# Attention and a gated MLP on one core: the first pair's loads in another order, a shared buffer for q, four buffers of split p

## The chip, the core and the metric

The kernel runs on one core of a Trainium2 chip. A core has five engines with their own instruction queues: TensorE (PE in the profile; its weight loads are PEld) multiplies matrices into PSUM, VectorE (DVE), ScalarE (ACT) and GpSimd (POOL) work on vectors, and SyncE (SP) issues most of the DMAs. Each engine works through its queue in order and waits on semaphores for the others. The metric is the device time of one execution in microseconds (us).

## The reference

Inputs are q, k and v of 4 batches x 8 heads x 1152 rows x 64 columns, and two weight matrices of 512 x 2048 and 2048 x 512, all f32. q and k are drawn with a spread near 0.79.

```python
q_pool = q.reshape(B, H, S // 2, 2, D).mean(axis=3)          # two neighbouring rows of q are one
scores = scale * np.matmul(q_pool, k.transpose(0, 1, 3, 2))  # 576 x 1152 for each head
scores = scores - np.max(scores, axis=-1, keepdims=True)
attn = np.exp(scores)
attn = attn / (np.sum(attn, axis=-1, keepdims=True) + 1e-09)
o = np.matmul(attn, v)
x = o.transpose(0, 2, 1, 3).reshape(B * 576, 512)            # heads side by side
h = x @ w_in
g = h * (1.0 / (1.0 + np.exp(-1.702 * h)))
out = g @ w_out
```

## The kernel before

The 32 heads are taken as 16 pairs, four for each batch. A pair has nine tiles of 128 rows of pooled q against 1152 columns of k (four of one head, "A", four of the other, "B", and one, "L", with 64 rows of each), so 144 score tiles in all.

**Pairs 0 to 3** (`WHOLE`, `WIDE`) are computed in f32. q and k are transposed on PE (`qk_tr`, L540) and copied out of PSUM in six parts (`qk_ev`), scores are f32 matmuls (L646), p is transposed on PE (`w_tr`, L768) and copied (`w_ev`), and p times v is L791. Meanwhile the two weight matrices are loaded in 32 pieces and made ready: `w_low` (L295) and `w_bits` (L299) on DVE, `w_exp` and `w_sign` on ACT, `w_mul` (L309) on POOL, a column sum on PE (`w_sum`, L314), and then `w_hi` and `w_lo` split them into two f16 parts.

**Pairs 4 to 15** use split operands: a value is an f16 high part plus an f16 rest, and a product is three f16 matmuls. q's row sums (`q_add`) are made on POOL, `q_hi` and `q_lo` write the two parts into `qn`, and `q_tr` transposes them by DMA; k goes the same way. For each tile: scores (L675); the row maximum and scaled copy `p` (`row_max`, L689); `lift` on the maximum; exponentials in place (`exps`, L696); `p_hi`, the f16 high part, into a buffer `hl` (L258 on ACT, L260 on DVE); `p_lo`, the rest, into the same buffer (L730); then one DMA transposes both into `pt` (`p_tr`, L743), and p times v follows on PE (L756). L258, L260 and L262 are lines of the helper `copy`, so many operations share them.

**The MoE part** runs in 9 blocks of 256 rows: h (L978), tanh on ACT, a gate on DVE, a split (`g_hi`, `g_lo`, L1003), and the second product (L1014). Blocks of a batch can start when its four pairs are done, and PE fills its waits with them. The last three blocks come after all attention.

**What sets the order.** Every step is added to a list (`plan.add`) with its engine, a cost, a rank, the steps that it follows, and the buffers that it takes and uses. `Plan.order` walks through it as a list scheduler: it picks the step that can start first by its costs, and among those within `wait` of that, the one of lowest rank. So the dictionary `rank`, the costs, `sizes` (how many buffers of a name there are) and `movable` (which steps may go to a second engine) set the order of each engine's queue; on the chip, semaphores alone decide when a step starts. `p` has three buffers, `hl` three, `pt` three, the scores one accumulator of three PSUM banks, and the loaded q, k and the parts `qn` one each. A step that takes a buffer waits for the last user of the one used before in the same place: `p_hi` waits for the transposition of the tile three before it.

The first pair's loads are issued by SP (q: first half, the two last parts, second half) and ACT (both heads of k, `k_load`); its row sums run on DVE. A load of the next pair's q waits until `q_add` has read the former one.

Of the kernel before, what the change touches and what calls it, by code (L numbers as in the profile page):

```python
# [141 lines left out]
def kernel(  # L142
# [26 lines left out]
    nc = tc.nc  # L169
# [18 lines left out]
        w1=1473.9738382899, w1_rate=812.7284009533, w2=2479.3934706835, w2_rate=62.2658245112,  # L188
        w1_cut=1764.9519973162, w1_cut_rate=0.0018904172, w2_cut=-269.851473856, w2_cut_rate=5.6062016033,
        v_max=1069.7920417805, load=-241.3418019351, prep=871.7951150424, max=-2026.5182514592,  # L190
        exp=640.8579795756, p_hi=-262.2674051923, p_lo=1525.5748408629, pv=1102.6265648828, x=557.4542312295,
        recip=1463.0570012603, w_tr=723.1050232894, w_ev=763.8780959185, g=-2229.8362745818,
        pv_b=-1120.3629115427, max_b=1656.4714364309, p_lo_b=1449.9352033366, prep_b=-1716.5596499645,
        v=1349.3135761977, lift=-444.2192073566,
# [21 lines left out]
    qn = [const.tile([128, 2, NJ, 128], F16, name=f"qn{i}") for i in range(1)]  # L216
# [126 lines left out]
    for i in range(32):  # L343
# [10 lines left out]
        plan.add(("w_low", i), "DVE", 0.335, r, lambda i=i: w_low(i), [("w_load", i)], use=[raw], two=True)  # L354
# [49 lines left out]
    def heads(x, g):  # L404
        return x[g.b, 2 * g.pr:2 * g.pr + 2]

    def k_load(g):
# [6 lines left out]
        for a in range(2):  # L414
            nc.scalar.dma_start(out=t[:, a], in_=heads(k, g)[a].rearrange("(p r) d -> p r d", r=KR))
# [704 lines left out]
    with tc.manual_schedule():  # L1120
# [6 lines left out]
        for t in qn:  # L1127
            nc.gpsimd.memset(t[:, 1, :, D:], 0.0)
# [32 lines left out]
```

## Time and profile before

| | us |
|---|---|
| median of 3 runs (lowest, highest) | 795.61 (793.12, 797.49) |
| profiled execution | 796.71 |
| span of the profiled execution | 795.0 |
| PE busy (share of the span) | 754.4 (95%) |
| DVE busy | 584.7 (74%) |
| ACT busy | 569.2 (72%) |
| POOL busy | 286.0 (36%) |

The span reaches from the first instruction to the last. Busy times are sums over the whole span, and the stages differ: pairs 0 to 3 end near 165 us, pairs 4 to 15 near 665, and the rest is MoE alone. A line of the profile names an engine, a source line, an operation and its tiles as out<-in; "idle before" is how long the engine stood still ahead of it, and the arrow says what ended that. A gap is read by asking which engine was late, and then why that engine was.

### The profile page before, as it was taken

The numbers are of one execution on the slowest core, as the hardware profiler recorded it, in microseconds if no ns is written. First come the engines' busy times: TensorE is split into PE (matmuls) and PEld (weight loads), VectorE is DVE, ScalarE is ACT, GpSimd is POOL, SyncE is SP. The second block draws the span as 40 slices with busy tenths as digits, with TensorE's granted clock in tenths as the row PEclk, the third lists the DMA queues.
The fourth block names the chain that finished last, engine by engine and source line by source line (L and its number), as shares of the span: only waits on it lengthen the run. The fifth ranks groups of instructions, "written<-read, shape, count | busy, mean of one in ns | idle before, by whom it ended". The sixth has DMA issues, their size and how long they took to land.

```text
span 795.0 us, 16660 instructions
## 1 busy us (share of the span) xinstructions
PE 754.4 (95%) x6716; PEld 509.3 (64%) x6716; DVE 584.7 (74%) x984; ACT 569.2 (72%) x929; POOL 286.0 (36%) x168
## 2 busy tenths in 40 slices
PE   5999999999998999999998998899999999999998
PEld 3565555656766677666675675666776677766664
DVE  5878999898887988788788887788787776222222
ACT  5988889789796878784777977776888886232322
POOL 3242242225746346334445543474364541000000
PEclk9999999999999999999999999999999999999999
DMA  9436073359999999999999999999999989010000
GB/s 302 171 136 217 30 247 112 113 120 189 208 206 202 189 225 185 215 201 214 180 209 217 208 179 196 236 205 200 194 226 187 173 127 177 1 28 2 27 1 26
DMA packets 335645, 128.75 MB, mean 162 GB/s; under 512 B 310736, under 2 KB 320976, under 8 KB 335568
## 3 DMA queue, kind: packets, MB, share of 16 engines
q1 hardware_dynamic: 335280, 127.10, 77.4%
q8 instruction: 52, 0.85, 0.4%
q10 hardware_dynamic: 288, 0.59, 0.3%
q14 instruction: 25, 0.20, 0.1%
HBM read 45.09 MB, written 4.72 MB: 63 GB/s over the span
## 4 chain that ended last, share of the span: by engine, by line
PE 61%; DMA 15%; DVE 10%; ACT 4%; issue 4%; POOL 3%; SPq 3%; POOLq 0%; DVEq 0%; ACTq 0%
PE h L978 16%; PE o L1014 15%; DMA pt<-hl 10%; PE s L675 7%; PE pv L756 7%; PE s L646 5%; DVE p L689 4%; PE o L768 4%; PE pv L791 4%; POOL hl L730 2%; ACT hl L258 2%; PE tr L803 2%; DMA raw<-in_moe_w_out_dram 1%; PE h L314 1%; SPq L743 1%
## 5 line engine op out<-in xcount | busy, mean ns | idle before, releaser
L730 POOL TENSOR_TENSOR hl<-p,hl 128x1152 f16<-128x1152 f32 x79 | 200.9, 2547 | 169.3 <-ACT hl L258 134.6
L689 DVE TENSOR_SCALAR_CACHE_REDUCE p<-s,e_s 128x1152 f32<-128x1152 f32 x144 | 203.3, 1412 | 34.5 <-PE s L675 24.0
L1014 PE MATMUL o<-wbuf,g 128*128 128x512 f16 x864 | 205.3, 379 | 1.2 <-DVE g L1003 1.2
L978 PEld LDWEIGHTS <-wbuf 128*128 128x128 f16 x1728 | 167.4, 98 | 41.9 <-issue 5.7
L696 ACT ACTIVATE p<-p,nm 128x1152 f32<-128x1152 f32 x144 | 179.8, 1249 | 12.5 <-DVE p L689 5.2
L258 ACT ACTIVATE hl<-p 128x1152 f16<-128x1152 f32 x99 | 114.4, 1157 | 43.3 <-DMA pt<-hl 41.6
L1014 PEld LDWEIGHTS <-g 128*128 128x128 f16 x864 | 83.2, 98 | 86.5 <-DVE g L1003 2.6
L675 PE MATMUL s<-kT,qT 128*128 128x384 f16 (+1 forms) x720 | 123.4, 326 | 10.3 <-DVE p L689 9.7
L978 PE MATMUL h<-x16a,wbuf 128*128 128x256 f16 x960 | 116.3, 273 | 0.7 <-DVE gf L992 0.7
L992 DVE SCALAR_TENSOR_TENSOR gf<-th,h 128x512 f32<-128x512 f32 x72 | 49.3, 684 | 83.7 <-ACT th L986 83.5
L986 ACT ACTIVATE th<-h,t_s 128x512 f32<-128x512 f32 x72 | 49.0, 680 | 77.8 <-PE h L978 77.0
L675 PEld LDWEIGHTS <-qT 128*128 128x128 f16 (+1 forms) x720 | 63.4, 100 | 54.1 <-issue 16.3
L978 PE MATMUL h<-wbuf 128*128 128x256 f16 x768 | 91.2, 273 | 2.7 <-DVE gf L992 2.7
L756 PEld LDWEIGHTS <-vhl 128*64 128x64 f16 x1944 | 83.7, 112 | 3.5 <-DMA pt<-hl 1.7
L756 PE MATMUL pv<-pt,vhl 128*64 128x256 f16 x1296 | 77.0, 276 | 2.5 <-DMA pt<-hl 2.5
L1003 DVE SCALAR_TENSOR_TENSOR g<-gf,g 128x512 f16<-128x512 f32 x72 | 62.3, 865 | 16.8 <-ACT g L258 16.6
L309 POOL TENSOR_TENSOR wbuf<-raw 128x512 f32<-128x512 f32 x32 | 35.4, 1115 | 82.7 <-ACT raw L305 82.7
L258 ACT ACTIVATE g<-gf 128x512 f16<-128x512 f32 x72 | 44.9, 623 | 22.0 <-DVE gf L992 22.0
L768 PE MATMUL o<-idf,p 128*128 128x128 f32 x324 | 49.2, 283 | 3.0 <-ACT pt L258 3.0
L646 PE MATMUL s<-kT,qT 64*128 64x512 f32 (+3 forms) x240 | 49.4, 523 | 1.5 <-DVE p L689 1.5
L730 DVE TENSOR_TENSOR hl<-p,hl 128x1152 f16<-128x1152 f32 x29 | 43.2, 1491 | 8.6 <-ACT hl L258 8.6
L768 PEld LDWEIGHTS o<-idf,p 128*128 128x128 f32 x324 | 35.2, 141 | 19.1 <-ACT pt L258 8.3
(105 smaller groups left out, 770.6 us busy)
## 6 DMA issues: line engine op xcount, KB each, us to landing
vraw<-in_v_dram SPq DMA_DIRECT2D x16, 576.0 KB, 5.1
kraw<-in_k_dram SPq DMA_DIRECT2D x15, 576.0 KB, 4.7
qraw<-in_q_dram SPq DMA_DIRECT2D x32, 256.0 KB, 3.5
raw<-in_moe_w_in_dram SPq DMA_DIRECT2D x16, 512.0 KB, 5.7
raw<-in_moe_w_out_dram SPq DMA_DIRECT2D x16, 512.0 KB, 4.9
out_dram<-osb SPq DMA_DIRECT2D x16, 256.0 KB, 2.6
pt<-hl SPq DMA_TRANSPOSE x96, 5.0
qraw<-in_q_dram SPq DMA_DIRECT2D x32, 32.0 KB, 3.3
```

What stands on the lines that cost most here:

```text
L258: nc.scalar.activation(out=out, in_=in_, func=ACTF.Copy, scale=1.0 if scale is None else scale)
L646: nc.tensor.matmul(out=ps[m, bank, 0:128 * (last - first)], lhsT=qT[h, (j - half) % NJ, m], rhs=kT[h, first:last].rearrange("p j c -> p (j ...
L675: nc.tensor.matmul(out=ps[m, c, 0:384], lhsT=st, rhs=T["kT", g.P][:, o:o + 3].rearrange("p r c -> p (r c)"), start=(l == 0), stop=(l == 1),)
L689: nc.vector.tensor_scalar(out=p, in0=s, scalar1=e_s[:, g.P:g.P + 1], scalar2=None, op0=ALU.mult, op1=ALU.min, accum_out=m)
L696: nc.scalar.activation(out=p, in_=p, func=ACTF.Exp, bias=T["nm", n], scale=-1.0, accum_out=sm)
L730: (nc.vector if e == "DVE" else nc.gpsimd).tensor_tensor(out=t[:, 1, :], in0=T["p", n].rearrange("p c f -> p (c f)"), in1=t[:, 0, :], op=A ...
L756: nc.tensor.matmul(out=ps[64 * a:64 * (a + 1), 0:w], lhsT=T["vhl", g.P][:, a, g.block[a][c], m], rhs=pt[:, l * KR + c, o:o + w], start=(pa ...
L768: nc.tensor.transpose(ps[:, 128 * i:128 * (i + 1)], T["p", n][:, c, 128 * i:128 * (i + 1)], idf)
L978: nc.tensor.matmul(out=h[:, e, :], lhsT=w1(2 * j + e, l, kk), rhs=x_rhs(blk, m, kk), start=(kk == 0 and l == 0 and m == 0), stop=(kk == KD ...
L992: nc.vector.scalar_tensor_tensor(out=gf, in0=T["th", blk, j], scalar=1.0, in1=T["h", blk, j].rearrange("p e n -> p (e n)"), op0=ALU.add, o ...
L1003: nc.vector.scalar_tensor_tensor(out=g[:, 1].rearrange("p e n -> p (e n)"), in0=T["gf", blk, j], scalar=2.0 ** -16, in1=g[:, 0].rearrange( ...
L1014: nc.tensor.matmul(out=o, lhsT=g[:, l, e, 128 * t:128 * (t + 1)], rhs=w2(fc, m), start=(fc == 0 and l == 0 and m == 0), stop=(fc == KFF - ...
```

## The change

1. The 25 numbers of `rank`, the `wait` and `slack` factors and `movable` have other values, so every queue comes out in another order. Steps that may run on a second engine are now `w_ev`, `x`, `lift`, `k_hi`, `q_hi` and `x_even` on DVE, and `p_lo` and `w_exp` on POOL.
2. `sizes`: `hl` has four buffers instead of three; `qn` is gone.
3. The parts of q are written over the loaded q (`qn(g)` is a view of `qraw`). The zeros in its second half, written once before, are written for each of pairs 4 to 15 by POOL (`q_zero`), and the loaded q is held until its transposition is done.
4. The first pair's loads: ACT issues one head of k and the second half of q, SP the first half of q, the last parts and the other head of k. The row sums follow as first half, second half, last.
5. `w_exp` and `w_low` of the first two weight pieces wait for the fourth copy of the first pair's transposed q and k (`qk_ev`, 0, 3).

```diff
     rank = dict(
-        w1=1473.9738382899, w1_rate=812.7284009533, w2=2479.3934706835, w2_rate=62.2658245112,
+        w1=1762.9849051451, w1_rate=0.191780252, w2=2169.0090854404, w2_rate=78.330453969,
...
-    movable = dict(DVE=('w_ev', 'x_hi', 'x_even', 'lift', 'qk_ev', 'p_hi', 'k_hi', 'v_hi'), POOL=('p_lo',))
+    movable = dict(DVE=('w_ev', 'x', 'lift', 'k_hi', 'q_hi', 'x_even'), POOL=('p_lo', 'w_exp'))
...
-        qraw=1, qs=1, kraw=1, kn=1, qn=1, kT=2, qT=2, vraw=2, vhl=1,
-        p=3, hl=3, pt=3, ptl=1, ...
+        qraw=1, qs=1, kraw=1, kn=1, kT=2, qT=2, vraw=2, vhl=1,
+        p=3, hl=4, pt=3, ptl=1, ...
...
-    qn = [const.tile([128, 2, NJ, 128], F16, name=f"qn{i}") for i in range(1)]
...
-            ("w_exp", i), "ACT", act(512) + 0.05, r, lambda e, i=i: w_exp(e, i), [("w_load", i)], use=[raw], two=True,
+            ("w_exp", i), "ACT", act(512) + 0.05, r, lambda e, i=i: w_exp(e, i),
+            [("w_load", i)] + ([("qk_ev", 0, 3)] if i < 2 else []), use=[raw], two=True,
...
+    def k_head(queue, g, a):
+        queue.dma_start(out=T["kraw", g.P][:, a], in_=heads(k, g)[a].rearrange("(p r) d -> p r d", r=KR))
...
-        for a in range(2):
-            nc.scalar.dma_start(out=t[:, a], in_=heads(k, g)[a].rearrange("(p r) d -> p r d", r=KR))
+        k_head(nc.scalar, g, 0)
...
-        for what, a in ("full", 0), ("last", 0), ("last", 1), ("full", 1):
+        for what, a in ("full", 0), ("full", 1), ("last", 0), ("last", 1):
...
-                nc.sync.dma_start(
+                (nc.scalar if g.P == 0 and a else nc.sync).dma_start(
...
+        if g.P == 0:
+            k_head(nc.sync, g, 1)
...
-        parts = [(0, 4, 0), (8, 9, 8), (4, 8, 4)] if g.P == 0 else [(0, 9, 0)]
+        parts = [(0, 4, 0), (4, 8, 4), (8, 9, 8)] if g.P == 0 else [(0, 9, 0)]
...
+    def qn(g):
+        t = T["qraw", g.P].rearrange("p j r d -> p (j r d)").bitcast(F16)
+        return t.rearrange("p (l j c) -> p l j c", l=2, c=128)
+
+    def q_zero(g):
+        nc.gpsimd.memset(qn(g)[:, 1, :, D:], 0.0)
...
-            plan.add(("q_tr", G), "SP", 2.9, r, lambda g=g: q_tr(g), [("q_lo", G)], take=[("qT", qt)], use=[qk], dma=1.84, tr=True)
+            plan.add(("q_zero", G), "POOL", 0.58, r, lambda g=g: q_zero(g), [("q_add", G)], use=[qr])
+            plan.add(("q_tr", G), "SP", 2.9, r, lambda g=g: q_tr(g), [("q_lo", G), ("q_zero", G)], take=[("qT", qt)], use=[qr], dma=1.84, tr=True)
...
-        for t in qn:
-            nc.gpsimd.memset(t[:, 1, :, D:], 0.0)
```

Line numbers after the change are some lines off those before (L258 is L257, L299 is L298, L438 is L443, L689 is L702, L743 is L756). Two places, on three engines, show what the order does. A number behind a name tells buffers apart; `o0` and `o1` are two PSUM banks, `raw` a loaded piece of a weight.

At the start of the program DVE's queue stood like this: the sums of q with the second half last, then bit operations of a first weight, then two copies of the transposed q and k.

```order
L438 TENSOR_TENSOR qs_130<-qraw_108 128x256
L438 TENSOR_TENSOR qs_130<-qraw_108 128x64 x2
L438 TENSOR_TENSOR qs_130<-qraw_108 128x256
L295 TENSOR_SCALAR raw_113<-raw_113 128x512
L260 COPY qT_149<-o1_140 128x512
L260 COPY kT_128<-o0_147 128x128
L299 SCALAR_TENSOR_TENSOR raw_113<-raw_113 128x512
L295 TENSOR_SCALAR raw_115<-raw_115 128x512
L295 TENSOR_SCALAR raw_117<-raw_117 128x512
L299 SCALAR_TENSOR_TENSOR raw_115<-raw_115 128x512
L299 SCALAR_TENSOR_TENSOR raw_117<-raw_117 128x512
```

Now it stands like this, up to the second row maximum.

```order
L443 TENSOR_TENSOR qs_128<-qraw_105 128x256 x2
L443 TENSOR_TENSOR qs_128<-qraw_105 128x64 x2
L294 TENSOR_SCALAR raw_111<-raw_111 128x512
L294 TENSOR_SCALAR raw_113<-raw_113 128x512
L298 SCALAR_TENSOR_TENSOR raw_111<-raw_111 128x512
L298 SCALAR_TENSOR_TENSOR raw_113<-raw_113 128x512
L702 TENSOR_SCALAR p_177,nm_176<-s_158,e_s_75 128x1152
L458 TENSOR_REDUCE qkv_194<-vraw_119 128x1
L702 TENSOR_SCALAR p_199,nm_198<-s_190,e_s_75 128x1152
```

The copies of the transposed q and k are gone from DVE, and two weights' bit operations stand together ahead of the first row maximum.

ACT's queue in the same place was this, from the loads on.

```order
L415 DMA kraw_105<-in_k_dram 128x576 x2
L258 ACT_TABLE_LOAD
L258 ACTIVATE kT_128<-o0_123 128x512
L258 ACTIVATE raw_113<-raw_113 128x512
L258 ACTIVATE qT_149<-o1_153 128x128
L305 ACTIVATE raw_113<-raw_113 128x512
L258 ACTIVATE kT_128<-o0_155 128x512
L258 ACTIVATE raw_115<-raw_115 128x512
L258 ACTIVATE raw_117<-raw_117 128x512
L305 ACTIVATE raw_115<-raw_115 128x512
L305 ACTIVATE raw_117<-raw_117 128x512
L258 ACTIVATE qT_149<-o1_175 128x512
```

And now, with the copies of all the first transposed parts on it:

```order
L409 DMA kraw_103<-in_k_dram 128x576
L425 DMA qraw_105<-in_q_dram 128x2x256
L257 ACT_TABLE_LOAD
L257 ACTIVATE kT_126<-o0_121 128x512
L257 ACTIVATE qT_145<-o1_138 128x512
L257 ACTIVATE kT_126<-o0_143 128x128
L257 ACTIVATE qT_145<-o1_148 128x128
L257 ACTIVATE raw_111<-raw_111 128x512
L257 ACTIVATE kT_126<-o0_150 128x512
L257 ACTIVATE raw_115<-raw_115 128x512
L304 ACTIVATE raw_111<-raw_111 128x512
L304 ACTIVATE raw_113<-raw_113 128x512
```

One load of k has become a load of q; the copies come first, and the first weight's exponent step stands between the fourth and the fifth.

SP's queue at a boundary of two pairs in the middle, before: the last transposition of a pair's p, those of the next pair's q and k, and then the loads for the pair after it.

```order
L743 DMA_TRANSPOSE ptl_3567<-hl_3515 128x18x128
L530 DMA_TRANSPOSE qT_3617<-qn0_73 128x18x128
L743 DMA_TRANSPOSE pt_3694<-hl_3615 128x18x128
L526 DMA_TRANSPOSE kT_3760<-kn_3584 128x18x128
L743 DMA_TRANSPOSE pt_3694<-hl_3696 128x18x128
L743 DMA_TRANSPOSE pt_3833<-hl_3743 128x18x128
L422 DMA qraw_3860<-in_q_dram 128x2x256
L427 DMA qraw_3860<-in_q_dram 64x128 x2
L422 DMA qraw_3860<-in_q_dram 128x2x256
L743 DMA_TRANSPOSE pt_3833<-hl_3806 128x18x128
```

The same boundary now:

```order
L756 DMA_TRANSPOSE ptl_3605<-hl_3526 128x18x128
L542 DMA_TRANSPOSE qT_3655<-qraw_3326 128x18x128
L538 DMA_TRANSPOSE kT_3702<-kn_3594 128x18x128
L756 DMA_TRANSPOSE pt_3783<-hl_3618 128x18x128
L756 DMA_TRANSPOSE pt_3783<-hl_3680 128x18x128
L756 DMA_TRANSPOSE pt_3854<-hl_3721 128x18x128
L425 DMA qraw_3888<-in_q_dram 128x2x256 x2
L430 DMA qraw_3888<-in_q_dram 64x128 x2
L756 DMA_TRANSPOSE pt_3854<-hl_3819 128x18x128
L414 DMA kraw_3940<-in_k_dram 128x2x576
```

The load of q stands about where it did, behind transpositions of p, but it now also waits for the landing of qT's transposition.

## Rows read from the trace of the kernel before

**Rows 1.** Windows: stretch, length; busy PE, PEld, DVE, ACT, POOL; clock, DMA, GB/s.

```profile
0.00:20.00 20.00, 11.56 (x44) 6.52 (x45) 10.60 (x29) 10.57 (x17) 6.21 (x12) 1.00 0.91 303
0.00:165.00 165.00, 152.40 (x1082) 92.63 (x1083) 140.01 (x262) 135.44 (x252) 49.34 (x51) 1.00 0.51 166
165.00:665.00 500.00, 475.81 (x4736) 331.53 (x4735) 410.03 (x672) 397.32 (x621) 235.36 (x115) 1.00 1.05 196
665.00:795.00 130.00, 126.22 (x902) 85.17 (x900) 34.63 (x52) 36.46 (x58) 1.34 (x2) 0.99 0.11 25
245.00:255.00 10.00, 8.72 (x82) 6.43 (x83) 6.56 (x11) 8.39 (x16) 6.17 (x4) 0.83 0.88 190
```

**Rows 2.** PE's timeline: start, length, instruction, [idle before <-releaser].

```profile
246.28 0.66 PE L803 MATMUL tr<-idf,w_r 128*64 128x128 f32 x8 [2.65 <-DVE w_r L714]
...
341.51 2.12 PE L978 MATMUL h<-wbuf 128*128 128x256 f16 x18 [1.61 <-DVE gf L992]
...
381.62 2.14 PE L978 MATMUL h<-wbuf 128*128 128x256 f16 x18 [1.07 <-DVE gf L992]
...
422.57 0.23 PE L465 MATMUL tr<-idb,qkv 128*128 128x128 bf16 x1 [1.46 <-DVE qkv L453]
...
554.90 1.14 PE L675 MATMUL s<-kT,qT 128*128 128x384 f16 x6 [1.67 <-DVE p L689]
614.85 1.14 PE L675 MATMUL s<-kT,qT 128*128 128x384 f16 x6 [1.01 <-DVE p L689]
```

**Rows 3.** Chain that ended last, ahead of 341.51: start, length, what.

```profile
331.08 7.90 DMA pt<-hl
...
339.00 0.03 ACT hl L258
```

**Rows 4.** Instructions writing `hl` on ACT, and what they waited for (us, times).

```profile
L258 ACT ACTIVATE hl<-p x99: 1146/1158/1166, 172.3 to 665.1; 128x1152 f16<-128x1152 f32 x99
...
  DMA pt<-hl: 41.6, 28
```

**Rows 5.** SP's transpositions of p: ns min/median/max; us to landing.

```profile
L743 SPq DMA_TRANSPOSE pt<-hl x96: 2403/2924/6049, 174.9 to 668.8; - x96
...
DMA to landing us min/median/max: 4.5/5.1/9.3
```

**Rows 6.** Timeline of the start, columns as in rows 2.

```profile
4.74 0.43 DVE L438 TENSOR_TENSOR qs<-qraw 128x256 f32<-128x256 f32 x1 [2.83 <-DMA qraw<-in_q_dram]
...
7.10 0.42 DVE L438 TENSOR_TENSOR qs<-qraw 128x256 f32<-128x256 f32 x1 [0.56 <-DMA qraw<-in_q_dram]
...
9.12 0.43 DVE L295 TENSOR_SCALAR raw<-raw 128x512 int32<-128x512 int32 x1 [1.59 <-DMA raw<-in_moe_w_in_dram]
...
10.20 0.48 PE L540 MATMUL o<-idf,qs 128*128 128x128 f32 x1 [1.93 <-DVE qT L260]
10.26 0.68 DVE L299 SCALAR_TENSOR_TENSOR raw<-raw 128x512 int32<-128x512 int32 x1
...
11.46 2.50 PE L646 MATMUL s<-kT,qT 64*128 64x512 f32 x6
...
14.07 1.41 DVE L689 TENSOR_SCALAR_CACHE_REDUCE p<-s,e_s 128x1152 f32<-128x1152 f32 x1
...
16.26 1.34 PE L646 MATMUL s<-kT,qT 64*128 64x512 f32 x6
```

**Rows 7.** POOL's product for the weights (L309): ns min/median/max.

```profile
L309 POOL TENSOR_TENSOR wbuf<-raw x32: 1033/1040/1911, 11.7 to 183.4; 128x512 f32<-128x512 f32 x32
```

**Rows 8.** Waits of SP, 165 to 665: total us, times, longest.

```profile
SPq L743 <- POOL hl L730: 60.2, 29, 4.6
```

**Rows 9.** Timeline near 300 us: `p_lo` on DVE and POOL.

```profile
289.51 1.36 DVE L730 TENSOR_TENSOR hl<-p,hl 128x1152 f16<-128x1152 f32 x1 [1.13 <-ACT hl L258]
...
307.78 2.92 POOL L730 TENSOR_TENSOR hl<-p,hl 128x1152 f16<-128x1152 f32 x1 [1.46 <-issue]
...
310.10 1.80 DVE L730 TENSOR_TENSOR hl<-p,hl 128x1152 f16<-128x1152 f32 x1
```

More of the change, by code (lines that the diff above doesn't have):

```diff
@@ L187 @@
     rank = dict(
-        w1=1473.9738382899, w1_rate=812.7284009533, w2=2479.3934706835, w2_rate=62.2658245112,
[L189 to L194, printed above, removed]
-    )
-    movable = dict(DVE=('w_ev', 'x_hi', 'x_even', 'lift', 'qk_ev', 'p_hi', 'k_hi', 'v_hi'), POOL=('p_lo',))
-    wait = dict(PE=0.010706, ACT=0.081524, DVE=0.106842, POOL=1.530524)
-    slack = dict(PE=0.215686, ACT=1.104301, DVE=1.062313, POOL=1.096162, SP=1.036393, stay=30.678012)
+        w1=1762.9849051451, w1_rate=0.191780252, w2=2169.0090854404, w2_rate=78.330453969,
+        w1_cut=1537.9653100599, w1_cut_rate=0.001, w2_cut=-300.19261431, w2_cut_rate=0.0127894989,
+        v_max=1564.5159800115, load=-136.4441868877, prep=538.4395457537, max=-2327.0038996143,
+        exp=1083.8893363201, p_hi=-164.5917704028, p_lo=1898.1955459363, pv=1138.7232330581,
+        x=374.0636095507, recip=1797.0485558552, w_tr=413.1535346346, w_ev=1098.6038986146,
+        g=-1757.8458041128, pv_b=-1318.1789094593, max_b=1766.9062966884, p_lo_b=1254.0433207475,
+        prep_b=-2024.1308908764, v=1829.336155201, lift=-353.9907322415,
+    )
+    movable = dict(DVE=('w_ev', 'x', 'lift', 'k_hi', 'q_hi', 'x_even'), POOL=('p_lo', 'w_exp'))
+    wait = dict(PE=0.016391, ACT=0.111231, DVE=0.006178, POOL=2.022565)
+    slack = dict(PE=0.243234, ACT=1.032672, DVE=1.073672, POOL=1.209907, SP=1.00598, stay=33.53572)
     sizes = dict(
-        qraw=1, qs=1, kraw=1, kn=1, qn=1, kT=2, qT=2, vraw=2, vhl=1,
-        p=3, hl=3, pt=3, ptl=1, xt=2, xf=2, raw=4, th=2, gf=2, g=3, osb=2, s=1, tr=1, pv=1, h=1, o0=1, o1=1,
+        qraw=1, qs=1, kraw=1, kn=1, kT=2, qT=2, vraw=2, vhl=1,
+        p=3, hl=4, pt=3, ptl=1, xt=2, xf=2, raw=4, th=2, gf=2, g=3, osb=2, s=1, tr=1, pv=1, h=1, o0=1, o1=1,
     )
@@ L619 @@
             plan.add(("q_hi", G), "ACT", act(1152, ptr=1), r, lambda e, g=g: q_hi(e, g), [("qkv_scale", G)],
-                     take=[("qn", qk)], use=[qs], two=True, or_on=on("q_hi", DVE=dve(1152, fast=True)))
-            plan.add(("q_lo", G), "DVE", dve(576) + 0.06, r, lambda g=g: q_lo(g), [("q_hi", G)], use=[qs, qk], two=True)
+                     use=[qs, qr], two=True, or_on=on("q_hi", DVE=dve(1152, fast=True)))
+            plan.add(("q_lo", G), "DVE", dve(576) + 0.06, r, lambda g=g: q_lo(g), [("q_hi", G)], use=[qs, qr], two=True)
+            plan.add(("q_zero", G), "POOL", 0.58, r, lambda g=g: q_zero(g), [("q_add", G)], use=[qr])
             plan.add(("k_hi", G), "ACT", act(1152, ptr=1), r, lambda e, g=g: k_hi(e, g), [("qkv_scale", G)],
```

13 lines of the change are left out of this document (7 added, 6 removed).

## The prediction

> **What bounds the kernel now.** I read the windows first, to see which engine is short of time in which stretch [rows 1]. TensorE (PE) is busy 152.4 of the first 165 us (the four pairs of heads computed in f32), 475.8 of the next 500 (the twelve pairs with split operands) and 126.2 of the last 130, where only MoE matmuls are left. All three rows have the granted clock at or next to 1.00, so the full level. The change leaves every matmul in place, so what can go is PE's idle time: 12.6 us in the first stretch, 24.2 in the second, 3.8 at the end, where the last output is copied and stored. Of the first 12.6 us, 8.4 lie in the first 20 us, so only 4.2 are left between 20 and 165.
>
> Then I read PE's own timeline for the longest gaps in the middle and what ended them [rows 2]: 2.65, 1.61, 1.07, 1.46, 1.67 and 1.01 us, 9.5 together, each ended by VectorE (DVE). A releaser is only the last link, so the chain of waits has to be followed further back. For the gap at 341.51 it goes through ScalarE (ACT) to a wait of 7.90 us on the transposing DMA that reads a buffer of split p, after which ACT may write the next high half [rows 3]. The chain of the other five passes through a transposition of split p in the same way, within about 12 us before the gap. ACT stands idle 41.6 us in 28 such waits [rows 4]: three buffers `hl` are too few, ACT works in order, and the tanh, the exponentials and the row sums of later tiles stand behind the blocked cast. The issuing queue sends one transposition in 2.92 us (median), and it lands 5.1 us after its issue [rows 5].
>
> **The start.** The sums of q begin with the first half at 4.74; the second half, issued after three other parts, is there at 7.10, and its sum takes 0.42. DVE then meets a weight's bit operation that is not fed until 9.12, ahead of the copy of qT, and PE loses 1.93 us to that copy at 10.20. The first score tile starts at 11.46, the first row maximum at 14.07, the second score tile at 16.26 [rows 6].
>
> In the new order the second half of q goes out on ACT's queue, behind one head of k, and the other head of k comes last on SP's. The five parts hold the same 1,152 KB, so I let the last of them land at 7.1 as before, now the second head of k. The second half of q follows the first by its 256 KB at the 303 GB/s of the first 20 us [rows 1], 0.9 us: 5.6. Sum 0.42, so 6.0; the transposes of q's first four blocks end near 6.5, the copy, now on ACT, near 7.2. The k block that straddles both heads waits for 7.1 and ends at 7.5, q's last block at 8.0, its copy at 8.3; k's last four take 1.1, so the first score tile starts at 9.2, 2.3 us earlier, and ends at 11.7 if it again takes 2.50.
>
> DVE now has the bit operations of two weights ahead of the first row maximum. The first weight still lands at 9.12, the second I put at 10.4. Its exponent step runs on GpSimd (POOL), for which I take the 1.04 us of POOL's product of the same size [rows 7], and with the two combining operations on DVE, 0.68 each, DVE is free near 12.4. So the row maximum comes 1.7 us earlier; with its 1.41 the second score tile can start at 14.0, 2.3 us earlier, since only two weight sums now stand ahead of it. I take **-2.2**. Bounds: -1.0 if the second weight lands 1.3 later than assumed, -3.0 if both land a little earlier. From 20 us on PE has hardly any idle time, so what is won here is kept.
>
> **The fourth buffer of split p.** With four, the cast of a tile waits for the transposition before the one that it waits for now, one issue of 2.92 us earlier. Each of the six gaps is shorter than that. So all 9.5 us could go, and with them the fall of the clock after the longest gap: 0.83 over 245 to 255 [rows 1] is, between the two levels, 3.4 us at 1.2 GHz, 1.7 us of work lost. Best case -11.2. In the worst case nothing goes, because the row's next engine is as late: DVE is busy 82% and ACT 79% of this stretch. I take half, **-5.5**: each chain has two links, ACT's wait for the buffer and DVE's work behind it, and the change shortens one.
>
> **Other order.** PE's score tiles have one accumulator, so between two of them must lie the row maximum, 1.41 us. Counting PE's matmuls between neighbouring score tiles, 5 places of the split half held under 1.7 us of work, now 2, and 25 places held under 2.5, now 17; in the f32 half the places under 1.7 go from 6 to 11, mostly by 0.1 to 0.3. The shortfall against 1.6 us falls by about 1.2 in the one and is unchanged in the other. I take **-1**, between -2.5 and +1.5.
>
> **At nothing.** The parts of q in the loaded q's place: the next q may be loaded only once qT's transposition has landed. At most pair boundaries two or three transpositions of p (2.92 each) stand on SP's queue between qT's and that load, and qT's, like p's, lands some 5.1 after its issue, so they cover it; without this cover SP would stand up to 3 us a pair. The zeros that were written once are now written in each of twelve pairs by POOL, each no longer than the 1.04 us of a product of about as many elements; POOL is busy 235 of 500 us there. Fifteen of 32 exponent steps move from ACT to POOL, which is busy 49 of 165 us in the first stretch; six subtractions of p move from POOL to DVE, nine casts from DVE to ACT, all balanced by smaller copies that move the other way. The gate on the first two weights costs nothing, since they land at 9.12, after the 8.3 that it asks for.
>
> **The sum.** 2.2 + 5.5 + 1 = 8.7. The profiled execution took 796.7 us, 1.7 more than its span, and 1.1 more than the median of 795.6. So 788.0 for that execution and **787** for the median.
>
> **Rivals.** (1) The wait moves to the next link: the fourth buffer is filled, but the queue of transpositions waits for POOL's subtraction, 60.2 us in 29 waits [rows 8]. For it: DMA share of 1.05 in the middle, and POOL's subtraction (2.92 us in [rows 9]) can take as long as the queue needs for a transposition. Against it: POOL is idle half of the stretch. Then only the start and the order remain: 795.6 - 3.2 = 792.4.
>
> (2) Slower: POOL's added work holds up DVE. At 310.10 DVE's subtraction of two operands takes 1.80 us, beside POOL's of 2.92 that began at 307.78 and ended 0.6 after DVE's began; without POOL beside it the same takes 1.36 at 289.51 [rows 9]. Fifteen exponent steps at 1.04 to 1.91 [rows 7] and twelve fills of at most 1.04 make 28 us of new POOL time; if half of that falls on DVE operations in the path of the scores, 14 us are added: 795.6 - 3.2 + 14 = 806. It decides once DVE's 25 idle us of the first stretch are used up. Against it: only operations that start at the same time are held, and then by a part. The Trainium skill, "SBUF — State Buffer", section "Who interferes with whom", makes it harder: the second port that DVE shares with GpSimd is a lock for the whole instruction, and the loser waits. By that rule every DVE operation with two inputs from SBUF that meets a step on POOL that reads SBUF waits for its whole rest; if each of the 28 us met one on the path, the time would be an estimated 820. The rows agree in kind, with 0.44 us lost of the 0.60 that the two ran together.
>
> (3) The change doesn't do what it says: q's loads come later behind qT, POOL meets its sum of q unfed, and p's subtractions queue behind it, so that the fourth buffer is never needed. At 0.5 us for each of eleven pairs, with the gain of the start alone: 795.6 - 2.2 + 5.5 = 799.
>
> **Chances.** Forecast 0.55 (its own range 781 to 792), the wait moves on 0.25, POOL holds DVE 0.12, q late 0.08. With 0.5%, 4 us, as what can be told from no change, faster ends at 791.6 and slower begins at 799.6. The forecast gives 0.51 faster and 0.04 same; the first rival 0.07, 0.17 and 0.01 slower; the second 0.01 same and 0.11; the third 0.05 and 0.03. Together 0.58, 0.27, 0.15. The range goes from 778, just past the three best cases together (795.6 - 3.0 - 11.2 - 2.5 = 778.9), to 799, which takes in rivals one and three.
>
> **What will show it.** First score tile near 9.2 and second near 14.0; ACT's idle time before the cast into `hl`, ended by the transposition, well under 20 us; PE idle in the middle stretch near 18 us instead of 24.2; no low clock near 250. Wrong, if that wait goes and PE's idle time in the middle stays (rival 1), if DVE's two-input operations in the first stretch are longer beside POOL (rival 2), or if POOL's wait for the loaded q grows (rival 3).

## The result, and the profile after

The changed kernel takes **800.4 us** (median of 14 runs, 797.8 to 805.5), the kernel before on the same chip 795.5 (14 runs, 793.1 to 797.7). The ratio is 1.0064, with the interval 1.0045 to 1.0082: slower by 0.6%. The forecast was 787.0, in 778 to 799, and faster. It was wrong in its sign, and the result lies outside the range.

The profiled execution took 798.9 us, its span 797.1. First the windows after, in the columns of [rows 1]; the last three are single stretches of 2 us.

```profile
0.00:20.00 20.00, 13.96 (x51) 7.85 (x52) 10.12 (x27) 10.42 (x18) 5.82 (x12) 0.91 0.88 305
0.00:165.00 165.00, 153.72 (x1082) 93.55 (x1083) 134.41 (x261) 134.72 (x247) 58.89 (x69) 0.99 0.53 171
165.00:665.00 500.00, 476.13 (x4725) 331.99 (x4723) 405.30 (x651) 412.23 (x641) 223.03 (x119) 0.99 1.04 195
665.00:795.00 130.00, 128.37 (x913) 86.16 (x910) 33.59 (x49) 37.22 (x58) 0.67 (x1) 1.00 0.08 21
245.00:255.00 10.00, 10.00 (x116) 7.53 (x114) 8.51 (x14) 8.19 (x17) 7.05 (x6) 1.00 1.15 225
16.00:18.00 2.00, 2.00 (x10) 1.57 (x10) 1.61 (x3) 0.70 (x4) 0.99 (x1) 0.50 1.01 375
206.00:208.00 2.00, 2.00 (x11) 1.40 (x10) 2.00 (x6) 1.58 (x5) 0.00 (x0) 0.50 0.74 155
330.00:332.00 2.00, 2.00 (x22) 1.73 (x20) 0.57 (x1) 0.03 (x1) 2.00 (x2) 0.50 0.94 313
```

TensorE's idle time in the middle stretch is 23.9 us; it was 24.2 [rows 1]. Over the whole span PE is idle 1.7 us less than before but busy 3.8 us more (758.2 instead of 754.4), with the same 6716 matmuls. The low clock near 250 [rows 1] is gone, and there are three others: near 16, 206 and 330 us the granted clock is 0.50, the level of 1.2 GHz, for 3.4 us each. Two such stretches more than before are, by estimate, 3.4 us of work, nearly all of the 3.8. So in this pair of profiles, whose spans are 2.1 us apart, the difference goes with the low clock and not with the idle time.

The waits between 165 and 665 us, before and then after (engine, line, what it waited for; us in total, times, longest):

```profile
POOL qs L438 <- DMA qraw<-in_q_dram: 34.8, 9, 9.1
...
PE s L675 <- DVE p L689: 9.7, 12, 1.7
...
PE pv L756 <- DMA pt<-hl: 2.5, 2, 1.4
```

```profile
POOL qs L443 <- DMA qraw<-in_q_dram: 50.5, 9, 9.5
...
ACT hl L257 <- DMA pt<-hl: 17.0, 10, 3.0
...
PE pv L769 <- DMA pt<-hl: 7.9, 5, 2.8
PE s L688 <- DVE p L702: 5.3, 8, 1.1
...
PE pv L769 <- DMA ptl<-hl: 2.0, 3, 1.0
```

ACT's wait for a buffer of split p fell from 41.6 us [rows 4] to 17.0, below the 20 of the forecast. What it held up did not get faster: PE waits less for row maxima and more, 9.9 us instead of 2.5, for the last transposition ahead of p times v, and POOL waits 16 us longer for q. The three longest gaps stand here, in PE's timeline after, in the columns of [rows 2]:

```profile
205.81 3.78 PE L991 MATMUL h<-x16a,wbuf 128*128 128x256 f16 x18 [3.34 <-DVE gf L1005]
...
328.64 4.80 PE L769 MATMUL pv<-pt,vhl 128*64 128x256 f16 x53 [2.84 <-DMA pt<-hl]
...
494.30 3.13 PE L769 MATMUL pv<-pt,vhl 128*64 128x256 f16 x53 [2.31 <-DMA pt<-hl]
```

SP's queue ahead of the second (issue, length) shows four parts of a q load just ahead of the transposition that `pv` needs:

```profile
321.38 1.05 SPq L425 DMA_DIRECT2D qraw<-in_q_dram  x2
322.48 1.14 SPq L430 DMA_DIRECT2D qraw<-in_q_dram  x2
323.72 3.19 SPq L756 DMA_TRANSPOSE pt<-hl  x1
```

At the start the first two score tiles came as forecast (9.00 and 14.26 us, against 9.2 and 14.0), and then the lead shrank. How close they came is in part luck: e3, e6, e10, e14 and e16, described below, have the same queues at the start, and there the first tile comes between 8.55 and 10.65 us and the second between 14.01 and 15.05. The starts of the first four score tiles, in us, from the timelines:

| | 1 | 2 | 3 | 4 |
|---|---|---|---|---|
| before | 11.46 | 16.26 | 19.12 | 22.95 |
| after | 9.00 | 14.26 | 18.39 | 21.77 |
| e3 (same start as after) | 8.98 | 14.01 | 17.52 | 20.90 |
| e6 (same start as after) | 10.42 | 14.95 | 18.46 | 21.84 |
| e2 | 12.59 | 17.40 | 20.33 | 24.15 |
| e7 | 10.14 | 14.13 | 19.55 | 24.86 |

### The profile page after: what moved, and what is told of

It reads as the page before. It is cut to its first block, busy times and chain, and to the rows that moved or that the text cites. A ratio compares the mean times of both kernels' runs of the same rounds, so it can differ in the third digit from the quotient of the medians.

```text
span 797.1 us, 16699 instructions
## 1 busy us (share of the span) xinstructions
PE 758.2 (95%) x6716; PEld 511.7 (64%) x6716; DVE 573.3 (72%) x960; ACT 584.2 (73%) x944; POOL 282.6 (35%) x188
## 4 chain that ended last, share of the span: by engine, by line
PE 58%; DMA 14%; DVE 11%; ACT 7%; issue 4%; POOL 3%; SPq 3%; POOLq 0%; DVEq 0%; ACTq 0%
PE o L1027 16%; PE h L991 16%; PE s L688 7%; DMA pt<-hl 6%; PE pv L769 6%; DVE p L702 4%; PE pv L804 4%; PE s L659 3%; PE o L781 3%; DMA raw<-in_moe_w_in_dram 2%; DMA ptl<-hl 2%; ACT p L709 2%; DMA vraw<-in_v_dram 2%; POOL hl L743 2%; SPq L756 1%
## 5 line engine op out<-in xcount | busy, mean ns | idle before, releaser
L743 POOL TENSOR_TENSOR hl<-p,hl 128x1152 f16<-128x1152 f32 x73 | 182.6, 2503 | 165.0 <-ACT hl L257 127.6
L702 DVE TENSOR_SCALAR_CACHE_REDUCE p<-s,e_s 128x1152 f32<-128x1152 f32 x144 | 203.5, 1413 | 45.0 <-PE s L688 31.1
L257 ACT ACTIVATE hl<-p 128x1152 f16<-128x1152 f32 x108 | 124.7, 1156 | 19.6 <-DMA pt<-hl 17.0
L688 PEld LDWEIGHTS <-qT 128*128 128x128 f16 (+1 forms) x720 | 62.7, 100 | 49.7 <-issue 14.3
L1016 DVE SCALAR_TENSOR_TENSOR g<-gf,g 128x512 f16<-128x512 f32 x72 | 56.5, 786 | 19.6 <-ACT g L257 19.6
L257 ACT ACTIVATE g<-gf 128x512 f16<-128x512 f32 x72 | 44.7, 621 | 20.9 <-DVE gf L1005 20.8
L743 DVE TENSOR_TENSOR hl<-p,hl 128x1152 f16<-128x1152 f32 x35 | 49.6, 1421 | 3.4 <-ACT hl L257 3.4
L308 POOL TENSOR_TENSOR wbuf<-raw 128x512 f32<-128x512 f32 x32 | 33.8, 1063 | 49.4 <-ACT raw L304 49.1
```

Source lines behind the costliest of these rows:

```text
L257: nc.scalar.activation(out=out, in_=in_, func=ACTF.Copy, scale=1.0 if scale is None else scale)
L688: nc.tensor.matmul(out=ps[m, c, 0:384], lhsT=st, rhs=T["kT", g.P][:, o:o + 3].rearrange("p r c -> p (r c)"), start=(l == 0), stop=(l == 1),)
L702: nc.vector.tensor_scalar(out=p, in0=s, scalar1=e_s[:, g.P:g.P + 1], scalar2=None, op0=ALU.mult, op1=ALU.min, accum_out=m)
L743: (nc.vector if e == "DVE" else nc.gpsimd).tensor_tensor(out=t[:, 1, :], in0=T["p", n].rearrange("p c f -> p (c f)"), in1=t[:, 0, :], op=A ...
L1016: nc.vector.scalar_tensor_tensor(out=g[:, 1].rearrange("p e n -> p (e n)"), in0=T["gf", blk, j], scalar=2.0 ** -16, in1=g[:, 0].rearrange( ...
```

## The experiments

Sixteen kernels ran, all with the same matmuls. "Idle" is PE's idle time from 165 to 665 us in the profiled run (500 less its busy time), "clock" the mean granted clock over all runs of the kernel. Each ratio is to the kernel before on the same chip, whose median was 795.5 to 796.7 us, so the ratio is what to compare. The idle time is that of a single execution, and it scatters: before, e2 and e7 have the same queues in this stretch and read 24.2, 19.3 and 21.1. The excerpts of the edits below are shortened, and the remarks behind # are not in the code.

| | us | ratio to before, interval | idle | clock |
|---|---|---|---|---|
| before | 795.5 | 1 | 24.2 | 0.997 |
| after | 800.4 | 1.0064 (1.0045, 1.0082) | 23.9 | 0.993 |
| e1 | 811.5 | 1.0205 (1.0177, 1.0233) | 36.4 | 0.986 |
| e2 | 794.2 | 0.9980 (0.9958, 1.0003) | 19.3 | 0.997 |
| e3 | 821.5 | 1.0337 (1.0309, 1.0364) | 36.3 | 0.981 |
| e4 | 816.0 | 1.0242 (1.0211, 1.0272) | 33.0 | 0.983 |
| e5 | 814.5 | 1.0214 (1.0183, 1.0246) | 35.6 | 0.986 |
| e6 | 800.6 | 1.0053 (1.0029, 1.0077) | 23.8 | 0.992 |
| e7 | 795.7 | 0.9973 (0.9950, 0.9995) | 21.1 | 0.994 |
| e8 | 791.9 | 0.9935 (0.9908, 0.9962) | 19.8 | 0.998 |
| **e9** | **789.3** | **0.9912 (0.9884, 0.9940)** | 16.6 | 0.999 |
| e10 | 799.3 | 1.0046 (1.0023, 1.0068) | 23.7 | 0.992 |
| e11 | 796.4 | 1.0003 (0.9979, 1.0026) | 22.7 | 0.996 |
| e12 | 822.1 | 1.0333 (1.0301, 1.0364) | 42.6 | 0.981 |
| e14 | 829.4 | 1.0418 (1.0388, 1.0448) | 45.1 | 0.987 |
| e15 | 833.8 | 1.0474 (1.0440, 1.0508) | 44.2 | 0.987 |
| e16 | 800.6 | 1.0064 (1.0035, 1.0093) | 24.4 | 0.994 |
| e17 | 796.2 | 0.9986 (0.9962, 1.0010) | 24.0 | 0.998 |

**Parts in the old order.** e1 and e5 keep before's queues and put q's parts in the loaded q's place; two loads of q, with what depends on them, must then move behind the transposition that frees it. e1 has four buffers of split p, e5 three.

```diff
-        T[key] = p.tile(..., bufs=sizes.get(tag, 8))
+        T[key] = p.tile(..., bufs=4 if tag == "hl" else sizes.get(tag, 8))   # e5: 3
...
-        for t, e in plan.order():
+        steps = plan.order()
+        for P in range(1, NPAIR):
...
+            load, tr = ("q_load", P), ("q_tr", P - 1)
+            if tr in at and at[load] < at[tr]:                               # so in pairs 5 and 6
...
+                steps = ([x for x in steps[:cut] if x[0]["name"] not in late]
+                         + [x for x in steps[:cut] if x[0]["name"] in late] + steps[cut:])
```

> PE, ACT and DVE in the order of the kernel before, q's parts in the loaded q's place, four buffers of split p (the order still made for three). If the fourth buffer is worth what the prediction took (5.5 us, at best 11): 785 to 791 us, ACT's wait for p's transposition down from 41.6 us to under 20, PE idle from 165 to 665 us near 18 instead of 24. If the wait only moves to the next link: 794 to 797, with ACT's wait down and PE's idle time as before. If holding the loaded q longer costs: 797 to 801, with POOL's wait for the loaded q up from 35.8 us.

> The same as e1 (q's parts in the loaded q's place, two q loads moved behind the transposition that frees their place, the order of before), but with three buffers of split p. It splits e1's loss. Theory A, the late q is all of it and the fourth buffer is worth nothing in an order that was written for three: 811, within 808 to 815, with the two gaps near 172 and 218 us of 6 and 8 us. Theory B, the fourth buffer won the forecast 5.5 us in e1 and the late q cost the more: 817 or above.

They lost 2.05% and 2.14%, and their intervals overlap: with q held in before's order, the fourth buffer took ACT's wait for it from 35.0 us (e5) to 1.9 (e1) and brought no time that can be told. e1's timeline shows the price at the first of the two pairs:

```profile
158.74 2.79 SPq L535 DMA_TRANSPOSE qT<-qraw  x1
163.42 0.40 SPq L421 DMA_DIRECT2D qraw<-in_q_dram  x1
...
168.24 1.40 POOL L437 TENSOR_TENSOR qs<-qraw 128x576 f32<-128x576 f32 x1 [21.55 <-DMA qraw<-in_q_dram]
...
171.70 1.54 PE L773 MATMUL o<-idf,p 128*128 128x128 f32 x6 [6.01 <-ACT pt L257]
```

The next load starts 4.7 us after qT's transposition is issued, POOL stands 21.55 us for it, and PE 6.01; the second pair costs 7.79 at 218.25.

e8 gives the fourth buffer without that, in before's order, with room taken from the MoE stage.

```diff
+        T[key] = p.tile(..., bufs={"hl": 4, "th": 3}.get(tag, sizes.get(tag, 8)))
+    w_r = w_d
-        gf = new("gf", ("gf", blk, j), [128, 512], F32, moe_pool())
+        gf = T["gf", blk, j] = T["th", blk, j]
```

> The order of before instruction by instruction, q's parts in their own buffer, and a fourth buffer of split p: the forecast's term by itself. The room comes from the MoE stage: the gate is written over tanh's output, in three buffers instead of two and two, and the reciprocals of the softmax sums over the sums. Theory A (the term of the forecast): ACT's 41.6 us of waits ahead of the cast into hl shrink and 5.5 us of TensorE's idle go, 790. Theory B (the wait moves to the next link: in an order written for three buffers the cast stands behind other work, and SP's transpositions land no earlier): ACT's wait nearly goes, TensorE's gaps stay, 795 to 797. Theory C, three buffers of tanh and gate hold the MoE stage: above 800, with waits for th or h.

It won 0.65%. ACT's instructions that write `hl` in e8 (in the form of [rows 4]), and the middle window:

```profile
L258 ACT ACTIVATE hl<-p x99: 1146/1150/1165, 172.1 to 662.2; 128x1152 f16<-128x1152 f32 x99
...
  DMA pt<-hl: 0.7, 1
```

```profile
165.00:665.00 500.00, 480.17 (x4764) 335.11 (x4764) 414.86 (x675) 399.03 (x624) 235.37 (x116) 0.99 1.05 197
```

Of the 41.6 us that ACT waited, 0.7 is left, and PE is idle 4.4 us less, which by itself is within the scatter of single profiles; the time of seven runs is not. The buffer is worth what the forecast gave it. The room taken from the MoE stage had nothing to give: in the profile before, from 165 to 665 us, the tanh waits for PE (9.8 us) and the gate for the tanh (14.3), neither for a free buffer.

e2 takes the first pair's loads and sums alone. e7 also puts the copies ahead of the first weights, as the change does, the first row maximum ahead of two of the weights' bit operations, and two weight sums on PE behind the second score tile.

```diff
+        k_head(nc.scalar, g, 0)                        # ACT: one head of k, q's second half
+        for what, a in ("full", 0), ("full", 1), ("last", 0), ("last", 1):   # the rest on SP
+        late([("w_exp", 0), ("w_low", 0)], ("qk_ev", 0, 3))    # e7 only, and the next two
+        late([("w_low", 2), ("w_bits", 1)], ("M", 0))
+        late([("w_sum", 1), ("w_load", 5)], ("S", 1))
```

> The kernel before with only the first pair's loads and sums in the new order; every other queue as before. If the landing of the second half of q set the start, the first score tile comes 1 to 2 us earlier (near 10) and the time is 793 to 794.5. If the copy of qT behind the first weight's bit operation on DVE set it, the first score tile stays at 11.2 to 11.5 and the time at 795 to 796.

> The kernel before with the first loads of e2 and, on top, the copies of the first qT and kT ahead of the first weight's bit operations on DVE and ACT, the first row maximum ahead of two of the weights' bit operations, and two of the weights' sums on TensorE behind the second score tile. In e2 the first score tile began at 12.59 us, because DVE's first weight operation waited for its transfer until 10.25 us. Theory A, the start is kept: first score tile at about 9.3 us, second at about 12 to 13, and the time 2 to 4 us below before, 792 to 794, 1 to 2 below e2. Theory B, what is won at the start is lost again in the next 20 us (exponentials on ACT, the lower clock, or later weights): as e2, 794 to 796.

e2's first tile comes later than before and its time is no worse; e7 leads by 2.1 us at the second tile and trails by 1.9 at the fourth. So the first score tile's time is no measure of the whole. e2 cannot be told from before, e7 hardly.

e9 puts e8 and e2 together.

> The order of before with e8's fourth buffer of split p (q's parts in their own buffer, room taken from the MoE stage) and e2's first loads. Theory A, the two parts add up: 4.9 us of e8 and 1.6 of e2, so about 790, within 788 to 792, with TensorE's idle time in 165 to 665 us near 20 and score tile 0 at about 12.6 us. Theory B, what the loads win at the start is taken back once ACT no longer waits for a buffer: as e8, 792.

789.3 us, the fastest of all, 7.3 below before on the same chip (796.6), and so below both kernels. The product of e2's and e8's ratios is 0.9915, measured is 0.9912; the intervals of e8 and e9 overlap, so what the loads add is not told. Its middle window:

```profile
165.00:665.00 500.00, 483.45 (x4800) 337.27 (x4799) 416.51 (x680) 401.11 (x629) 233.46 (x116) 1.00 1.06 200
```

**Orders.** e3 is the changed kernel with three buffers in place of four, its queues untouched; e4 has the new rules with the old numbers (`rank`, `movable`, `wait`, `slack`); e12 the old rules and numbers planned for four buffers; e11 the new numbers and four buffers with q's parts in a place of their own, planned so; e10 the changed kernel's queues with q's parts in a place of their own and the loads of pairs 5 and 6 earlier.

```diff
-  bufs=sizes.get(tag, 8)
+  bufs=3 if tag == "hl" else sizes.get(tag, 8)                # e3
-        w1=1762.9849051451, ...
+        w1=1473.9738382899, ...                               # e4, all numbers of before
-        p=3, hl=3, ...
+        p=3, hl=4, ...                                        # e12
-  [("q_lo", G), ("q_zero", G)], take=[("qT", qt)], use=[qr]
+  [("q_lo", G)], take=[("qT", qt)], use=[qk]                  # e11, with qn=1 in sizes
+        for load, ahead in (("q_load", 5), ("q_tr", 4)), (("q_load", 6), ("T", 40)):   # e10
+            steps.insert(at[ahead], steps.pop(at[load]))
```

> The changed kernel with its order untouched, but three buffers of split p. If the buffer is worth something in the new order: 803 to 810 us, ACT's wait for p's transposition up from 17 us to 40 or more. If it is not: 799 to 802, as the changed kernel.

> The changed kernel with the old rank, movable, wait and slack, so that the scheduler makes another order from the new rules. If the new numbers are what costs: 790 to 796 us. If the rules (q held longer, gate on the first weights, first loads) cost: 799 to 803. If any order that is made for other rules loses, since numbers and rules belong together: anywhere above 800.

> The kernel before with its own numbers and its own q buffer, but planned for four buffers of split p, where e8 kept the order that was planned for three. Theory A, the gain of the fourth buffer comes from the place itself: as e8 or better, 788 to 793. Theory B, the order as planned anew with numbers fitted to three buffers loses more than the buffer wins: 800 to 815, with TensorE's gaps at score tiles and low parts of p early or late by several us.

> The changed kernel with the planner's rule for q as before (a buffer of its own, so an order planned without the hold), all new numbers and the four buffers kept. Theory A, the hold costs because it forces the order: below the changed kernel, 790 to 796. Theory B, an order is as good as the numbers were fitted to its rules, and any rule changed without refitting loses the 15 to 20 us that e3 and e4 lost: 810 to 820.

> The changed kernel's order, but q's parts in a buffer of their own (one memset at the start instead of one per pair on POOL; room from the MoE stage as in e8), and the q loads of two pairs ahead of the transposition of the pair before, as they stood before the change. Theory A, the shared place of q is what costs under the new order too: POOL's wait for q's load (54.3 us in all) falls below 40, the gap at 205 us goes, and the time is 793 to 796. Theory B, under the new order q's place costs nothing any more (its loads stand behind the transposition that frees them by the order itself), and the new order as such is what is slower: 799 to 801.

e12 against e8 is the plainest pair: the same operations and buffers, once in the order planned for three buffers, once planned anew, and 30 us between them. e4 lost 20 us against before, e3 25. So an order that does not go with its buffers and numbers costs far more than any single part won. e10 equals the changed kernel: in its queues the held place of q costs nothing any more, since they already put the loads behind. e11 comes out at the upper edge of its first forecast: planned without the hold, the order is 0.6% faster than the changed kernel's, and still it only comes level with before.

**What the new order loses.** e6 moves what stands ahead of the three longest gaps: two q loads one transposition later, and a low part of p on DVE behind the gate.

```diff
+        late([("L", 41)], ("gate", "h", 0, 3))
+        for P, n, m in (9, 66, 69), (13, 102, 104):
+            late([("q_load", P)], ("T", n))
+            late([("q_add", P), ("q_zero", P)], ("L", m))
```

> The changed kernel with three local moves: two of the q loads (the ones at 321 and 487 us) one transposition later in SP's queue, their sums on POOL behind the casts' low parts that wait there, and one low part of p on DVE behind the gate at 201 us. Theory A, the changed kernel's time was lost at these places and in the lower clock behind two of them: the gaps of 3.34, 2.84 and 2.31 us fall below 1 us, the granted clock no longer falls near 206 and 330 us, and with 7 us of gaps and some 3 us of lower clock gone the time is 790 to 793. Theory B, the waits only move on to the next link (q arrives late for its own pair, or the next transposition waits): gaps of the same sum come back within some 20 us, and the time is 799 to 802.

e6's timeline in the same places:

```profile
207.66 0.66 PE L816 MATMUL tr<-idf,w_r 128*64 128x128 f32 x8 [2.16 <-DVE w_r L727]
...
330.28 0.23 PE L470 MATMUL tr<-idb,qkv 128*128 128x128 bf16 x1 [1.58 <-DVE qkv L449]
332.13 0.23 PE L470 MATMUL tr<-idb,qkv 128*128 128x128 bf16 x1 [1.61 <-DVE qkv L458]
333.84 0.29 PE L470 MATMUL tr<-idb,qkv 128*128 128x128 bf16 x1 [1.49 <-DVE qkv L458]
335.17 1.12 PE L688 MATMUL s<-kT,qT 128*128 128x384 f16 x3 [1.03 <-DVE p L702]
...
498.42 1.17 PE L688 MATMUL s<-kT,qT 128*64 128x384 f16 x12 [3.13 <-DVE p L702]
```

The gaps of 2.84 and 2.31 us are gone; within 7 us the maxima of the late q and a score tile take their place, 5.7 and 3.1 us. The low clock near 206 us is gone, too, and the one near 330 is twice as long (6.8 us from 333 on). Idle and time stay.

From pair 5 on, e14 and e15 put each `pv` behind the next score tile, in the changed order and in e9's; e16 and e17 draw up to two MoE products ahead of `pv` instead.

```diff
+                    late([("pv", P, u, 0)], nxt[0])          # e14, e15: nxt[0] is the next S
+                        steps.insert(to + n, steps.pop(i))   # e16, e17: i a step h or o, to that of pv
```

> The changed kernel with every product of p and v of the pairs from 5 on one score tile later in TensorE's order, so that a score tile of 1.14 us stands ahead of each wait for the last transposition. Theory A, this wait is what the new order loses: pv's wait for the transposition falls from 9.9 us to 3 or less, TensorE's idle in 165 to 665 us from 23.9 to 17 or less, and the time is 793 to 796. Theory B, TensorE is held by the chain of tiles as a whole (score, row maximum, exponential, cast, low part, transposition), and a wait taken from pv comes back at a score tile or at what reads pv: the idle stays at 22 to 25 and the time at 799 to 803.

> e9 (the order of before, a fourth buffer of split p, the first loads) with the same shift of pv by one score tile. There pv waits only 1.8 us for transpositions. Theory A of e14: at most 1.8 us to win, 787 to 790. Theory B: nothing to win, and products and their readers that come later cost 1 to 4 us: 790 to 794.

> The changed kernel with 26 of the MoE stage's products (0.65 us each, at most two at a place) drawn ahead of the products of p and v of the pairs from 5 on; the score tiles keep their order among themselves. Theory A, pv's waits for the last transposition (9.9 us) are what the new order loses: they fall to 5 or less (two of the three largest, at 455 and 494 us, are covered), TensorE's idle in 165 to 665 us falls from 23.9 to about 19, and the time is 795 to 797. Theory B, the chain of tiles as a whole sets the pace: the score tiles behind pv come later by what was drawn ahead, and the time is 799 to 806.

> The same rule in e9's order, where pv waits 1.8 us for transpositions. Theory A: 1 us to win at most, 788 to 790. Theory B: 790 to 797, as the score tiles come later.

e14's and then e16's waits between 165 and 665 us:

```profile
PE s L688 <- DVE p L702: 35.8, 33, 3.7
...
PE pv L769 <- DVE xf L846: 0.5, 1, 0.5
```

```profile
PE s L688 <- DVE p L702: 10.6, 15, 1.6
PE pv L769 <- DMA pt<-hl: 3.9, 3, 3.0
...
PE pv L769 <- DMA ptl<-hl: 0.9, 2, 0.5
```

In e14 no wait of `pv` for a transposition is left; two score tiles now stand side by side with one accumulator between them, and the row maxima cost more than was saved. That says nothing of what `pv`'s wait is worth. e16 does: the wait fell from 9.9 to 4.8 us, that for row maxima rose from 5.3 to 10.6, and the time is the changed kernel's. e17 lost 6 to 7 us against e9 by the same rule. The score tiles are what the row maxima, exponentials and casts follow from; what was put ahead of them in these four kernels was paid back.

One stretch tells the planned orders apart, picked out of the profiles afterwards: 300 to 345 us, here after and in e9 (columns of [rows 1]).

```profile
300.00:345.00 45.00, 39.72 (x381) 27.52 (x379) 34.24 (x53) 36.84 (x57) 18.43 (x12) 0.96 1.11 204
```

```profile
300.00:345.00 45.00, 45.00 (x478) 32.81 (x476) 40.07 (x65) 37.51 (x59) 22.41 (x10) 1.00 1.10 208
```

PE is idle 5.3 us there after and not at all in e9. In the kernels with before's queues there (before, e1, e2, e5, e7, e8, e9 and, but for the drawn products, e17) it is 0.0 to 1.9 us; in the nine others with a newly planned order (after, e3, e4, e6, e10, e11, e12, e14, e16) 4.5 to 9.4, and in all of these but e11 a part of it runs at the low clock. The nine come from four orders: after's, which six of them share or vary, and those of e4, e11 and e12. e15, before's queues with `pv` later, has 5.1.

## Why the prediction was wrong

**The step that failed is "Other order", taken as -1 between -2.5 and +1.5.** e9 has the buffer and the loads with before's queues elsewhere, so the rest of the change, its new order with q held, costs the quotient: 1.0064 / 0.9912 = 1.015, 12 us, where the forecast had a gain of 1. Of these, 5 lie between the orders planned with and without q held (after against e11) and 7 between before's order and the new numbers planned for four buffers (e11 against e9), each within 2 to 3 us. Each is one planned order against another, so neither is shown to be the price of a rule as such. I had counted matmuls between neighbouring score tiles. That view does not contain the queues of SP, POOL and ACT, whose order changed everywhere, and the range came from that one count.

In the profiles, after is 9.6 us of span longer than e9 (797.1 against 787.5): 4.3 of it is PE's busy time (758.2 against 753.9) and the rest idle, of which the middle stretch has 7.3 more and the first 1.7 less. The busy part goes with the clock: three low stretches against one ahead of the last microseconds, and over all runs 0.993 against 0.999, by estimate 0.006 x 800 = 4.7 us. Of the idle time of the middle stretch, 5.3 of the 7.3 us lie at 300 to 345.

**The fourth buffer, -5.5: right by itself.** e8 measured 0.65%, about 5 us, ACT's wait went, and PE's idle time fell by 4.4. Rival 1, the wait moves to the next link, does not hold there, although SP waits as long for POOL's subtraction as in [rows 8] (59.8 us in 31 waits). In the changed kernel its sign appeared all the same, ACT's wait down and PE's idle time as before; but there the order is planned around the buffer, and with three e3 lost 21 us more. The list of longest gaps that the best case was made of is not complete: PE's timeline before also has 1.43 (496.68), 1.35, 1.17, 1.12, 1.10 and 1.08 us, and two of these (1.43 and 1.12) end with the landing of a transposition.

**q in the loaded q's place, at nothing: wrong in before's order, right in the new one, and not free in the planning.** The cover of transpositions stood at nine of the eleven loads; at those of pairs 5 and 6 before's queue has the load ahead of qT's transposition, which I had not looked up, and e1 shows gaps of 6.0 and 7.8 us there. Rival 3's sign, POOL's longer wait for q, appeared (34.8 to 50.5), but it is the order that makes it: without the hold, in e10, the wait is 50.8, and the time is the changed kernel's.

**The start, -2.2 and kept: the two tiles right, "kept" wrong, mostly by the clock.** Of 2.0 us of lead at the second tile 1.2 are left at the fourth. Most of what was lost went with the low clock from 14.7 to 18.1 us, which stretched the second tile. PE's timelines after and of e6, which has the same queues and a granted clock of 1.00 there:

```profile
14.26 2.13 PE L659 MATMUL s<-kT,qT 64*128 64x512 f32 x6 [0.73 <-DVE p L702]
```

```profile
14.95 1.34 PE L659 MATMUL s<-kT,qT 64*128 64x512 f32 x6 [0.73 <-DVE p L702]
```

From the second tile to the fourth, before takes 6.69 us, e3, e6 and e16, at 1.00, take 6.88 or 6.89, and after takes 7.51: the order loses 0.2, the clock 0.6. The forecast's sum had no term for a low clock at the start. Over the first 20 us PE is idle 2.4 us less than before, about what was forecast; the low clock gives 1.7 back, and from 20 to 165 us PE is idle 1.1 more. A lead can also be lost in the queues: e7 lost 2.1 us by the fourth tile, PE standing 1.47 for ACT's exponentials ahead of the third, with a low clock from 19.3 on.

**POOL's added work, rival 2: not seen.** The moved exponent steps took 0.77 us each where I took 1.04, the fills 0.58, so the new work is 18 us and not 28. In the first 165 us, where the exponent steps run, PE is idle 11.3 us, less than before, and the step on DVE that combines two parts of a weight takes 0.73 us on average instead of 0.77. One collision of DVE and POOL cost a gap (last section), and it is of an old operation. The argument against this rival was wrong all the same: an operation need not start together with POOL's to be held, and it is not held by a part only (last section). And the estimate of 820 counted the fills among the steps that read SBUF, which they don't.

**Open.** Which of the new numbers makes the chain of tiles slower is not settled, nor why the newly planned orders lose at 300 to 345 us: the moves of e6 and e16 took away the longest gaps and half of `pv`'s wait, and the idle time came back within the chain. Nor did any run separate the clock from the gaps ahead of it, and the 4.7 us stay an estimate: after's own runs at the two ends of its clock, 0.997 and 0.989, took 799.0 and 802.4, 3.4 us apart where the same estimate has 6.4.

## What to carry to other kernels

A re-planned order is a term of its own, and its range is wide: with nearly the same work, planned orders here ran from 795.5 to 822 us, and none of the newly planned ones was faster than before. Price a new resource in the old order first (e8: three changed lines), and only then ask whether a new order is wanted. And where a chain of tiles sets the pace, a gap that is filled is not a gap that is won: read the sum of the idle time and not the gap, and over more than one profile, since the same queues read 19.3 and 24.2 us here.

## What the runs showed of the hardware

A two-operand subtraction on DVE beside one on POOL waited much longer than in [rows 9]. Timeline after (start, length, instruction), POOL's and then DVE's:

```profile
200.59 3.35 POOL L743 TENSOR_TENSOR hl<-p,hl 128x1152 f16<-128x1152 f32 x1
...
201.64 3.52 DVE L743 TENSOR_TENSOR hl<-p,hl 128x1152 f16<-128x1152 f32 x1
205.08 0.68 DVE L1005 SCALAR_TENSOR_TENSOR gf<-th,h 128x512 f32<-128x512 f32 x1
```

Alone it takes 1.36 [rows 9], so 2.16 us were lost of the 2.30 in which the two overlapped, and the gate behind it set PE's gap of 3.34 at 205.81. In [rows 9] it was 0.44 of 0.60. It is no matter of the new order: the kernel before has one of the same size, here from its timelines, POOL's and then DVE's.

```profile
269.13 2.89 POOL L730 TENSOR_TENSOR hl<-p,hl 128x1152 f16<-128x1152 f32 x1
```

```profile
269.71 3.53 DVE L730 TENSOR_TENSOR hl<-p,hl 128x1152 f16<-128x1152 f32 x1
```

Nine of the 29 such subtractions on DVE in the kernel before begin while an instruction of POOL runs that reads SBUF, and each takes 1.36 us and what is left of POOL's, less 0.06 to 0.15. The Trainium skill, "SBUF — State Buffer", section "Who interferes with whom", says that the one that issues first has the shared port pair for its whole instruction and the other is blocked: these traces agree within 0.15 us. After, the collision cost one gap of 3.3 us, not the path as a whole: e6 kept the gate clear of it, and nothing was won.

The granted clock fell at the same places in kernels of the new order, near 206 and 330 us in after, 210 and 332 in e10, 208 and 334 in e16, in after right behind the gaps of 3.34 and 2.84 us. e9 has one such stretch, near 375 behind a gap of 1.03 us, and e8 two, near 377 behind a gap of 1.03 and near 497 at the end of one of 2.31; the gap of 2.31 at 494.30 in after has none behind it. So the length of the gap alone does not tell whether the clock falls.
